# Contiguous operands for TensorE, v turned on the chip, and a new instruction order in a fused attention and gated-MLP kernel

## The chip, the cores and the metric

One core of a Trainium2 chip; the runs were made on four chips, so kernels are compared by their ratio to the kernel before in the same rounds. The metric is the device time of one execution, in microseconds (us), median of several runs. The kernel before takes 230.99 us (229.94 to 232.09, 3 runs).

## The reference, cut to what matters

```python
# q, k, v: (8 batches, 8 heads, 576, 64), fp32
scores = scale * q @ k^T                     # heads 0-3: band of 32; heads 4-7: band of 32 in steps of 4
attn   = softmax(where(mask, scores, -1e9))
x      = concat_heads(attn @ v)              # (8, 576, 512)
h      = gelu_tanh(x @ w_in)                 # 512 -> 1024
u, v_  = split(h)                            # 512 and 512
v_n    = (v_ - mean) / sqrt(var + 1e-6) * g_ln
v_s    = w_sg @ v_n + b_sg                   # "gating", over the 576 positions
out    = x + (u * v_s) @ w_out               # the residual is x itself
```

Of the kernel before, what the change touches and what calls it, by code (L numbers as in the profile page):

```python
# [11 lines left out]
FP32 = mybir.dt.float32  # L12
# [13 lines left out]
def _masks() -> np.ndarray:  # L26
    out = np.zeros((KB, 2, S), dtype=np.float16)
    p = np.arange(KB)[:, None]
    for a in range(NB):
        j = QB * a - HALO + p  # L30
        i = QB * a + np.arange(QB)[None, :]
        out[:, 0, QB * a:QB * a + QB] = (j >= 0) & (i >= j) & (i - j < 32)
    u = np.arange(128)[None, :]
    main = (u >= p) & (u - p < 32)
    i, j = 128 + np.arange(16)[None, :], 96 + p % 48
    tail = [(p // 48 == r) & (i >= j) & (i - j < 32) for r in range(2)]
    out[:, 1] = np.concatenate([x for r in range(2) for _ in range(2) for x in (main, tail[r])], axis=1)
    return out
# [3 lines left out]
ew iLQP:1 iLKP:1 iLQD:0 R:1:0:0 iLKD:0 R:1:0:1 w:27@2 S:1:0:1@0,1 iLQP:0 iLKP:0 iMSK iLVP:0 iLVH:0 iLVD:0  # L42
iLVT:0:1 iLVT:0:0 iLWV S:1:0:0@2,3 iLQD:1 iLWSG R:0:1:0 R:0:1:1 R:0:0:0 E:1:0:1:1 E:1:0:0:0 E:1:0:1:0
R:0:0:1 iLKD:1 S:0:1:1@1,2 E:1:0:0:1 S:0:1:0@0,3 E:0:1:0:1 E:0:1:1:1 M:0:3 E:0:1:1:0 E:0:1:0:0 iID iLWU
M:1:0 M:1:1 M:0:2 S:0:0:1@3,2 S:0:0:0@1,0 E:0:0:0:1 E:0:0:1:0 iBG AS:1:0@0 E:0:0:1:1 M:0:1 LN:1:0 iLKD:2
E:0:0:0:0 VC:0 AS:0:1@3 M:0:0 w:5@2 AS:0:0@2 w:3@1 AV:0:0:1@0 LN:0:0 LN:0:1 EX:0:0 EX:0:1 gw AV:0:0:0@1
NX:0:0:0 NX:0:0:1 w:4@2 AV:0:1:1@2 iLQD:2 AV:0:1:0@3 NX:0:1:0 NX:0:1:1 zv:0:4@1 R:1:1:0 Gz:0:2 st:0:4
zv:0:2@0 zv:0:3 Gz:0:1 zv:0:0@3 iLQP:2 sc:0 sa:0 rs:0:2 st:0:2 st:0:3 zv:0:1 Gz:0:0 ew st:0:1 st:0:0 R:1:1:1
WP:0:0 WP:0:1 w:13@1 W:0:2@2 S:1:1:1@1,0 E:1:1:1:1 rs:0:0 E:1:1:1:0 rs:0:1 vn:0:4 W:0:4@3 WC:0:2 iLKP:2
S:1:1:0@2,0 WC:0:4 E:1:1:0:0 vn:0:1 E:1:1:0:1 gw vn:0:0 W:0:0@3 zu:0:0@1 W:0:1@2 WC:0:0 M:1:3 WC:0:1 W:0:3@0  # L50
zu:0:2@3 Gu:0:2 M:1:2 vn:0:3 vn:0:2 WC:0:3 BG R:2:1:0 Gu:0:0 zu:0:1@2 Gu:0:1 zu:0:3@3 R:2:1:1 Gu:0:3 ew
AS:1:1@1 LN:1:1 sgr:0:1@2,0 sgu:0:1 EX:1:0 EX:1:1 VS:0:1 sgu:0:3 VS:0:3 sgr:0:0@3,1 sgu:0:2 VS:0:2 R:2:0:1
GA:0:2 w:2@2 S:2:1:1@2,0 E:2:1:1:1 sgu:0:0 E:2:1:1:0 GA:0:1 S:2:1:0@1,0 E:2:1:0:1 E:2:1:0:0 R:2:0:0 w:6@2
S:2:0:0@2,0 iLVH:1 iLVP:1 GA:0:3 VC:1 VS:0:0 GA:0:0 AV:1:0:1@1 E:2:0:0:0 E:2:0:0:1 NX:1:0:1 iLWO M:2:2 M:2:3
iLVT:1:0 AV:1:0:0@3 S:2:0:1@2,0 E:2:0:1:0 M:2:0 E:2:0:1:1 out:0:0@1 out:0:1 iLVT:1:1 O:0:0 out:0:4@2 O:0:2
M:2:1 NX:1:0:0 AS:2:0@0 LN:2:0 iLVD:1 AV:1:1:0@3 AS:2:1@1 LN:2:1 AV:1:1:1@2 EX:2:1 out:0:2@0 NX:1:1:0
NX:1:1:1 zv:1:0@3 iLVT:2:1 zv:1:1 EX:2:0 gw Gz:1:0 zv:1:2@1 zv:1:3 Gz:1:1 iLKP:3 out:0:3 R:3:0:1 iLVT:2:0
iLVD:2 st:1:1 O:0:1 st:1:0 zu:1:2@2 iLVP:2 iLVH:2 Gu:1:2 zv:1:4@3 iLQP:4 iLKD:4 st:1:2 Gz:1:2 iLKP:4 rs:1:0
st:1:3 vn:1:1 st:1:4 AV:2:1:1@1 NX:2:1:1 VC:2 vn:1:0 AV:2:1:0@0 zu:1:3@2 iLQD:3 zu:1:0@3 sc:1 sa:1 iLQP:3
AV:2:0:0@1 NX:2:1:0 rs:1:1 iLKD:3 NX:2:0:0 Gu:1:3 rs:1:2 iLVT:3:0 AV:2:0:1@0 zu:1:1@2 Gu:1:1 NX:2:0:1  # L60
zv:2:4@1 iLVH:3 vn:1:3 R:4:1:1 vn:1:2 R:4:0:1 R:4:0:0 zv:2:2@0 Gz:2:2 zv:2:3 Gu:1:0 iLVP:3 Gz:2:1 st:2:2
zu:2:1@2 zv:2:0@1 zv:2:1 Gz:2:0 vn:1:4 st:2:3 zu:2:0@3 Gu:2:0 zu:2:3@0 Gu:2:3 R:3:0:0 Gu:2:1 R:3:1:1
zu:2:2@1 sgr:1:0@3,0 Gu:2:2 ew sgu:1:0 st:2:4 R:3:1:0 S:4:0:1@2,1 E:4:0:1:0 VS:1:0 st:2:0 sgu:1:2 VS:1:2
E:4:0:1:1 iD:0:2 GA:1:0 sgr:1:1@3,2 sgu:1:3 iD:0:1 VS:1:3 GA:1:2 S:3:1:0@1,0 sgu:1:1 rs:2:1 GA:1:3 VC:3
E:3:1:0:1 E:3:1:0:0 iLVT:4:1 sc:2 iLVD:3 VS:1:1 iLVT:3:1 sa:2 GA:1:1 S:4:0:0@2,0 E:4:0:0:1 E:4:0:0:0 iLQD:4
st:2:1 S:3:1:1@1,3 E:3:1:1:1 E:3:1:1:0 out:1:2@0 S:3:0:1@2,3 M:4:1 iD:0:0 rs:2:0 M:3:3 vn:2:1 vn:2:0 iLVH:4
iLQD:5 M:3:2 out:1:3 rs:2:2 vn:2:2 iLVP:4 vn:2:4 vn:2:3 iLQP:5 iLKD:5 E:3:0:1:1 S:3:0:0@1,3 E:3:0:1:0
E:3:0:0:1 E:3:0:0:0 M:3:1 out:1:0@2 M:3:0 out:1:1 M:4:0 O:1:1 AS:3:1@3 R:4:1:0 O:1:0 sgr:2:0@1,0 LN:3:1
iLKP:5 EX:3:1 sgu:2:0 AS:3:0@2 VS:2:0 AV:3:1:1@3 LN:3:0 sgu:2:2 NX:3:1:1 VS:2:2 EX:3:0 AV:3:0:0@2 AS:4:0@1
LN:4:0 out:1:4@3 NX:3:0:0 O:1:2 AV:3:1:0@0 NX:3:1:0 AV:3:0:1@1 NX:3:0:1 VC:4 GA:2:2 sgr:2:1@3,2 sgu:2:1  # L70
S:4:1:0@0,1 VS:2:1 EX:4:0 E:4:1:0:1 E:4:1:0:0 R:5:0:0 GA:2:1 sgu:2:3 GA:2:0 S:4:1:1@3,1 E:4:1:1:1 VS:2:3
E:4:1:1:0 gw zv:3:2@0 R:5:0:1 GA:2:3 M:4:2 zv:3:3 Gz:3:1 zv:3:0@1 zv:3:1 Gz:3:0 iD:1:2 iD:1:0 zv:3:4@3
iD:1:1 M:4:3 AV:4:0:0@2 Gz:3:2 ew NX:4:0:0 iLVH:5 AV:4:0:1@0 iLVD:4 NX:4:0:1 AS:4:1@1 LN:4:1 out:2:2@3
R:5:1:0 R:5:1:1 st:3:4 st:3:3 S:5:0:1@2,0 out:2:3 iLVT:4:0 E:5:0:1:1 iLVT:5:1 iLVD:5 out:2:0@1 iLQD:6
E:5:0:1:0 EX:4:1 O:2:1 sc:3 S:5:1:0@0,2 st:3:1 E:5:1:0:0 iD:2:1 iLQP:7 st:3:0 E:5:1:0:1 out:2:1 AV:4:1:1@3
O:2:0 NX:4:1:1 sa:3 rs:3:2 out:2:4@0 AV:4:1:0@2 O:2:2 iLKD:7 NX:4:1:0 rs:3:0 S:5:0:0@1,3 iD:2:2 E:5:0:0:1
E:5:0:0:0 st:3:2 rs:3:1 iLVP:5 iLVT:5:0 zu:3:0@0 S:5:1:1@2,3 zv:4:2@1 iLKD:6 E:5:1:1:1 M:5:1 M:5:0 zv:4:0@3
vn:3:0 iD:2:0 vn:3:4 vn:3:2 vn:3:1 R:7:0:0 E:5:1:1:0 gw zv:4:3 M:5:2 M:5:3 vn:3:3 Gu:3:0 Gz:4:1 zu:4:0@2
Gu:4:0 zv:4:1 Gz:4:0 zu:3:3@0 Gu:3:3 zv:4:4@1 Gz:4:2 ew st:4:3 st:4:0 st:4:4 iLQP:6 iLKP:6 sgr:3:0@2,3 sc:4
st:4:1 iLVD:6 AS:5:1@0 AS:5:0@1 LN:5:0 LN:5:1 EX:5:1 EX:5:0 gw iLQD:7 rs:4:0 sgu:3:0 VS:3:0 sgu:3:2 sa:4  # L80
st:4:2 VS:3:2 rs:4:2 zu:3:2@1 GA:3:0 Gu:3:2 VC:5 sgr:3:1@0,2 sgu:3:1 VS:3:1 sgu:3:3 VS:3:3 zu:3:1@3 Gu:3:1
GA:3:2 AV:5:1:1@1 AV:5:1:0@0 iLVT:6:1 AV:5:0:1@2 NX:5:1:1 iLVD:7 NX:5:1:0 vn:4:4 AV:5:0:0@3 NX:5:0:1
zu:4:3@1 zu:4:2@0 Gu:4:3 iLVT:7:0 zu:4:1@2 NX:5:0:0 Gu:4:1 Gu:4:2 GA:3:1 zv:5:2@1 zv:5:3 zv:5:0@3 zv:5:1
rs:4:1 Gz:5:0 iLKP:7 vn:4:1 vn:4:3 R:6:0:1 GA:3:3 out:3:2@2 vn:4:0 R:6:1:1 Gz:5:1 out:3:3 O:3:1 R:6:1:0
zu:5:1@0 zv:5:4@3 Gu:5:1 out:3:4@1 iLVT:7:1 vn:4:2 R:6:0:0 st:5:0 Gz:5:2 ew R:7:1:0 st:5:2 st:5:4 sc:5
S:6:0:0@2,0 E:6:0:0:0 E:6:0:0:1 O:3:2 st:5:3 out:3:0@3 out:3:1 O:3:0 st:5:1 R:7:1:1 rs:5:0 sa:5 sgr:4:1@2,0
sgu:4:3 VS:4:3 sgu:4:1 VS:4:1 S:6:1:1@1,3 E:6:1:1:0 E:6:1:1:1 gw zu:5:3@0 zu:5:0@2 iLVT:6:0 rs:5:2 Gu:5:0
GA:4:1 rs:5:1 vn:5:4 GA:4:3 vn:5:1 vn:5:3 sgr:4:0@1,3 sgu:4:2 VS:4:2 vn:5:2 vn:5:0 GA:4:2 sgu:4:0 VS:4:0
zu:5:2@2 Gu:5:3 sgr:5:1@0,3 sgu:5:1 Gu:5:2 ew S:6:0:1@2,1 E:6:0:1:1 GA:4:0 VS:5:1 sgu:5:3 E:6:0:1:0 R:7:0:1
M:6:1 out:4:2@0 VS:5:3 iLVP:6 S:6:1:0@1,2 iD:3:2 iLVH:6 out:4:3 M:6:0 GA:5:1 E:6:1:0:0 out:4:0@3 E:6:1:0:1  # L90
VC:6 out:4:1 iD:3:1 iD:3:0 M:6:3 GA:5:3 O:4:1 O:4:0 sgr:5:0@1,2 M:6:2 AS:6:1@0 LN:6:1 sgu:5:0 S:7:0:1@3,0
VS:5:0 sgu:5:2 EX:6:1 GA:5:0 E:7:0:1:0 S:7:1:1@1,3 E:7:0:1:1 E:7:1:1:1 VS:5:2 out:4:4@0 O:4:2 E:7:1:1:0
AS:6:0@2 LN:6:0 iLVH:7 iLVP:7 AV:6:1:0@3 GA:5:2 EX:6:0 iD:4:0 out:5:0@0 S:7:1:0@1,2 E:7:1:0:1 iD:4:2 iD:4:1
NX:6:1:0 AV:6:0:0@3 NX:6:0:0 out:5:1 E:7:1:0:0 S:7:0:0@2,3 VC:7 M:7:3 M:7:2 E:7:0:0:1 M:7:1 E:7:0:0:0 O:5:0
M:7:0 out:5:2@1 out:5:3 AV:6:1:1@3 O:5:1 NX:6:1:1 AV:6:0:1@2 NX:6:0:1 out:5:4@0 O:5:2 AS:7:0@3 AV:7:0:1@1
AV:7:0:0@0 AS:7:1@2 LN:7:0 EX:7:0 LN:7:1 EX:7:1 gw zv:6:0@3 zv:6:1 Gz:6:0 NX:7:0:1 NX:7:0:0 AV:7:1:0@2
AV:7:1:1@1 NX:7:1:0 NX:7:1:1 zv:6:2@0 st:6:0 st:6:1 rs:6:0 zv:6:3 zv:7:2@2 Gz:6:1 st:6:2 st:6:3 vn:6:1
zv:6:4@1 Gz:6:2 vn:6:0 zv:7:4@3 zv:7:3 rs:6:1 vn:6:2 st:6:4 vn:6:3 Gz:7:1 Gz:7:2 st:7:3 st:7:4 sc:7 zu:7:3@0
zv:7:0@1 zv:7:1 Gz:7:0 st:7:1 sa:7 st:7:0 zu:7:2@2 Gu:7:2 rs:7:0 zu:7:0@3 zu:6:3@1 Gu:7:3 zu:6:1@2 Gu:6:3
Gu:6:1 zu:6:0@0 zu:6:2@1 Gu:6:0 st:7:2 Gu:7:0 sc:6 sa:6 rs:6:2 vn:6:4 zu:7:1@2 rs:7:1 rs:7:2 sgr:6:1@0,3  # L100
vn:7:0 vn:7:2 Gu:7:1 vn:7:1 sgu:6:1 VS:6:1 Gu:6:2 vn:7:3 sgr:6:0@2,1 vn:7:4 sgu:6:3 VS:6:3 GA:6:1 sgu:6:0
# [8 lines left out]
def kernel(  # L110
# [110 lines left out]
    def ld_mask():  # L221
        nc.sync.dma_start(masks, MSK.ap())
# [335 lines left out]
```

## The kernel before: the parts that the change and the argument touch

Positions are kept in residue order (position modulo 4 first), since the dilated heads need it. The order of all instructions is one long list of short names (the plan), played from left to right; each engine is given its own instructions in that order. `E` is an exp, `M` a mask product, `AV` attention times v, `S` the scores, `vn` a norm, `sgr`/`sgu` the gating, `w:n` are n filler matmuls of zeros, `@2,3` names the PSUM slots.

```python
def E(b, g, hf, x):                      # g = 0: band heads, g = 1: dilated heads
    nc.scalar.activation(PTb[...][:, :, HS*hf:HS*hf+HS], live["pss", b, g, hf][x][:, :, 0:HS], AF.Exp, scale=0.125)

def AV(b, g, x):                         # band heads: PT is read in steps of four
    ...
        nc.tensor.matmul(o[:, :, 24*(s%3):24*(s%3)+24], v_, PT[:, QB*s:QB*s+QB].rearrange("p (m u) -> p u m", u=4), ...)

def out_(b, ti):                         # the residual: a matmul onto the identity, every second column of PSUM
    ...
        nc.tensor.matmul(po[:, ti % 2, 256*(g4//2):256*(g4//2)+256].rearrange("p (w x) -> p x w", x=2)[:, g4 % 2, :],
                         xT[:, g4, ts], ident16, start=False, stop=(g4 == 3))

def vn(b, ti):                           # norm, on VectorE
    nc.vector.tensor_scalar(dst, vv, mean, rstd, AO.subtract, AO.mult)

def ld_vp(b):                            # v in rows of 64 elements, one queue (SyncE)
    nc.sync.dma_start(vst[HALO:KB], v[b][0:4].rearrange("h (a p) d -> p (h a) d", p=QB))
```

The softmax here doesn't subtract the row's maximum and nothing guards it: scores larger than these inputs give would overflow.

## Time and profile before

| | before |
|---|---|
| time | 230.99 us |
| span of the profiled run | 229.2 us |
| TensorE / VectorE / ScalarE busy | 209.8 / 171.2 / 147.3 us |
| fillers among TensorE's work | 60 matmuls, 16.8 us |
| first large projection, first gating matmul | 29.0 us, 46.1 us |

The first fence is the table of stretches of the kernel before (length, then busy time of PE, PEld, DVE, ACT and POOL, clock, DMA share, GB/s); the second is ScalarE's largest group up to the first gating matmul at 46.08 us.

```profile
40.00:60.00 20.00, 19.07 (x289) 12.87 (x288) 18.29 (x30) 13.79 (x21) 5.28 (x9) 0.93 0.90 140
60.00:80.00 20.00, 20.00 (x277) 12.44 (x274) 15.72 (x30) 13.49 (x19) 5.44 (x12) 1.00 0.77 126
80.00:100.00 20.00, 19.30 (x312) 12.38 (x311) 18.42 (x35) 16.84 (x25) 10.90 (x18) 1.00 0.98 180
```

```profile
L292 ACT ACTIVATE PT<-pss 128x576 f16<-128x576 f32 x16 | 9.4, 654 | 13.4 <-PE pss L288 13.3
```

Sixteen exps, those of two batches, are done before the first gating, and ScalarE still stood 13.4 us for scores. They had room there.

### The profile page before, as it was taken

How to read it: one execution, taken by the hardware profiler on the slowest of the kernel's cores; microseconds unless marked ns; L12 is line 12 of the kernel's file. 1: busy time of each engine (PE TensorE's matmuls, PEld its weight loads, DVE VectorE, ACT ScalarE, POOL GpSimd, SP SyncE). 2: the span in 40 equal slices, each digit the busy share in tenths (PEclk: the TensorE clock that was granted, in tenths of full speed). 3: DMA queues.
4: the chain of work that ended last, by engine and by line, in shares of the span. 5: the costliest groups of instructions: out<-in, count | busy, mean ns of one | idle time of the engine just before them, and what ended most of it. 6: DMA issues, size and time to landing. Idle time of an engine off the chain costs nothing.

```text
span 229.2 us, 6969 instructions
## 1 busy us (share of the span) xinstructions
PE 209.8 (92%) x3020; PEld 131.5 (57%) x3020; DVE 171.2 (75%) x314; ACT 147.3 (64%) x201; POOL 67.8 (30%) x131
## 2 busy tenths in 40 slices
PE   7627896998999999999999999999999999999990
PEld 2223444765657566565565676666656655766650
DVE  2487478898768999899879989988955668686400
ACT  2068658678685598778979973756788785721231
POOL 8244057602017061922029364050000003420000
PEclk9955999799999999999999999999999999999998
DMA  8999997993917979998849999026076430000354
GB/s 157 205 216 212 208 205 136 171 158 57 219 22 102 209 220 171 142 190 124 246 69 223 215 216 195 8 44 212 3 125 159 159 114 3 0 1 3 114 169 128
DMA packets 45326, 31.68 MB, mean 138 GB/s; under 512 B 30048, under 2 KB 36704, under 8 KB 45296
## 3 DMA queue, kind: packets, MB, share of 16 engines
q0 software_dynamic: 13984, 14.95, 41.6%
q1 hardware_dynamic: 31312, 16.29, 29.4%
q8 instruction: 23, 0.38, 0.7%
q14 instruction: 7, 0.06, 0.1%
HBM read 36.75 MB, written 9.44 MB: 202 GB/s over the span
## 4 chain that ended last, share of the span: by engine, by line
PE 71%; DMA 9%; DVE 9%; ACT 4%; POOL 2%; issue 2%; ACTq 1%; DVEq 0%; POOLq 0%
PE po L465 13%; PE pg L443 11%; PE pz L367 11%; PE pu L421 10%; PE po L468 6%; DMA qkp<-in_k_dram 5%; PE pss L288 4%; DMA qkd<-in_k_dram 4%; PE pav L310 4%; PE psu L338 3%; DVE vs L449 2%; PE po L475 2%; PE pg L436 2%; PE pav L321 2%; PE pb L507 2%
## 5 line engine op out<-in xcount | busy, mean ns | idle before, releaser
L292 ACT ACTIVATE PT<-pss 128x576 f16<-128x576 f32 x64 | 38.0, 651 | 24.7 <-PE pss L288 24.6
L421 PE MATMUL pu<-xT,w_in 128*128 128x288 f16 x256 | 35.4, 292 | 0.0
L443 PE MATMUL pg<-wsgT,vn 128*128 128x288 f16 x256 | 35.4, 287 | 0.0
L465 PE MATMUL po<-w_out,gat 128*128 128x512 f16 x128 | 33.5, 384 | 0.0
L449 DVE SCALAR_TENSOR_TENSOR vs<-pg,g_col,b_bc 128x576 f16<-128x576 f32 x32 | 25.5, 804 | 9.3 <-PE pg L443 9.2
L367 PE MATMUL pz<-w_in,xT 128*128 128x512 f16 x128 | 29.7, 380 | 0.0
L421 PEld LDWEIGHTS <-w_in 128*128 128x128 f16 x256 | 25.0, 100 | 7.9 <-issue 0.3
L487 ACT COPY osb<-po 128x1024 f32<-128x1024 f32 x16 | 16.2, 1016 | 19.9 <-PE po L468 18.7
L443 PEld LDWEIGHTS <-vn 128*128 128x128 f16 x256 | 23.2, 98 | 9.6 <-issue 3.8
L426 ACT ACTIVATE u<-pu 128x576 f16<-128x576 f32 x32 | 19.9, 650 | 12.7 <-PE pu L421 12.5
L406 POOL TENSOR_SCALAR rs<-mv 128x2 f32<-128x2 f32 (+1 forms) x24 | 7.0, 292 | 67.2 <-DVE mv L393 62.4
L297 DVE TENSOR_TENSOR PT<-PT,masks 128x1152 f16<-128x1152 f16 x32 | 22.8, 748 | 1.4 <-ACT PT L292 1.3
L388 DVE BATCH_NORM_STATS2 st<-vv 128x6 f32<-128x512 f32 x32 | 21.5, 671 | 3.2 <-ACT vv L378 3.1
L378 ACT ACTIVATE vv<-pz 128x1024 f32<-128x1024 f32 x16 | 16.3, 1025 | 9.3 <-PE pz L367 7.2
L412 DVE TENSOR_SCALAR vn<-vv,mv,rs 128x512 f16<-128x512 f32 (+1 forms) x40 | 19.2, 507 | 3.2 <-POOL rs L407 3.2
L367 PEld LDWEIGHTS <-xT 128*128 128x128 f16 x128 | 12.0, 99 | 13.3 <-issue 0.6
L468 PE MATMUL po<-ident,xT 128*128 128x128 f16 x128 | 19.2, 304 | 0.0
L352 DVE TENSOR_TENSOR xT<-pav,rsum 128x576 f16<-128x576 f32 x16 | 11.6, 752 | 8.6 <-PE pav L310 5.0
L407 POOL TENSOR_TENSOR rs<-rs,mhalf 128x2 f32<-128x2 f32 (+1 forms) x24 | 17.4, 723 | 2.0
L507 PE MATMUL pb<-zeros 128*128 128x512 f16 x60 | 16.8, 433 | 1.2 <-DVE zeros L170 1.2
L465 PEld LDWEIGHTS <-gat 128*128 128x128 f16 x128 | 12.3, 107 | 9.2 <-issue 0.4
L468 PEld LDWEIGHTS <-xT 128*128 128x128 f16 x128 | 13.2, 118 | 7.6
(68 smaller groups left out, 311.5 us busy)
## 6 DMA issues: line engine op xcount, KB each, us to landing
vst<-in_v_dram SPq DMA_DIRECT2D x8, 576.0 KB, 9.0
qkp<-in_q_dram POOLq DMA_DIRECT2D x8, 288.0 KB, 5.9
qkp<-in_k_dram POOLq DMA_DIRECT2D x8, 288.0 KB, 8.0
qkd<-in_q_dram POOLq DMA_DIRECT2D x8, 288.0 KB, 6.3
qkd<-in_k_dram POOLq DMA_DIRECT2D x8, 288.0 KB, 7.5
vm<-in_v_dram POOLq DMA_DIRECT2D x8, 256.0 KB, 6.7
out_dram<-osb SPq DMA_DIRECT2D x8, 256.0 KB, 3.5
out_dram<-osb SPq DMA_DIRECT2D x8, 224.0 KB
```

Of the source, the lines that this page charges most:

```text
L292: nc.scalar.activation(PTb[4 * (b % 2) + 2 * g + x][:, :, HS * hf:HS * hf + HS], live["pss", b, g, hf][x][:, :, 0:HS], AF.Exp, scale=0.125)
L297: nc.vector.tensor_tensor(PT, PT, masks[:, p // 2, :].unsqueeze(1).broadcast_to([KB, 2, S]), AO.mult)
L367: nc.tensor.matmul(pz[:, ti % 2, :], xT[:, g4, 128 * ti:128 * ti + 128], w_in16[:, g4, DH:DFF], start=(g4 == 0), stop=(g4 == 3))
L388: nc.vector.bn_stats(s, vvs[(3 * b + i) % 4][:, c, :])
L412: nc.vector.tensor_scalar(vns[b % 2][:, ti, 0:n], vvs[(3 * b + i) % 4][:, c, 0:n], live["mv", b, i][:, c, 0:1], live["rs", b, i][:, c, :], ...
L421: nc.tensor.matmul(pu[:, j, 0:HS], w_in16[:, g4, 128 * ph:128 * ph + 128], xT[:, g4, HS * j:HS * j + HS], start=(g4 == 0), stop=(g4 == 3))
L426: nc.scalar.activation(us[b % 2][:, ph, :].rearrange("p (j w) -> p j w", j=2), live.pop(("pu", b, ph))[:, :, 0:HS], AF.Gelu_apprx_tanh)
L443: nc.tensor.matmul(pv[:, j, 0:HS], vns[b % 2][:, kp, 128 * ph:128 * ph + 128], wsgT16[:, kp, HS * j:HS * j + HS], start=False, stop=(kp == 3))
L449: nc.vector.scalar_tensor_tensor(vs.rearrange("p (j w) -> p j w", j=2), live.pop(("pg", b, ph))[:, :, 0:HS], g_col[:, ph:ph + 1], b_bc.rea ...
L465: nc.tensor.matmul(po[:, ti % 2, :], gat[:, ph, ts], w_out16[:, ph, :], start=(ph == 0), stop=False)
L468: nc.tensor.matmul(po[:, ti % 2, 256 * (g4 // 2):256 * (g4 // 2) + 256].rearrange("p (w x) -> p x w", x=2)[:, g4 % 2, :], xT[:, g4, ts], i ...
L507: nc.tensor.matmul(pb[:, 0, :], zeros[:, 0:128], zeros, start=True, stop=True)
```

## The change

Its intent: make every operand of TensorE contiguous (the residual's output, the band heads' PT), load v of the first two batches in whole rows instead of short pieces and turn it on the chip, make the first loads smaller, share the norms between VectorE and ScalarE, and play all of it in a new order. The diff, cut to its core:

```diff
 def E(b, g, hf, x):
+    if g == 0:                                        # exp writes residue order
+        dst = dst.rearrange("p h (u m) -> p h u m", u=4)
+        src = src.rearrange("p h (m u) -> p h u m", u=4)
 def AV(b, g, x):
-                        PT[:, QB * s:QB * s + QB].rearrange("p (m u) -> p u m", u=4),
+                        PT[:, HS * (s // 3):HS * (s // 3) + HS].rearrange("p (u m) -> p u m", u=4)[
+                            :, :, 24 * (s % 3):24 * (s % 3) + 24],
 def out_(b, ti):
-                nc.tensor.matmul(po[:, ti % 2, 256 * (g4 // 2):256 * (g4 // 2) + 256].rearrange(
-                        "p (w x) -> p x w", x=2)[:, g4 % 2, :], xT[:, g4, ts], ident16, ...)
+                nc.tensor.matmul(po[:, ti % 2, 128 * g4:128 * g4 + 128], xT[:, g4, ts], ident16, ...)
+def WO():                                             # w_out's columns permuted once, on GpSimd
+def O(copy):                                          # the eviction undoes the order; on ScalarE or VectorE
+def ld_v(b, g):                                       # whole rows, two batches only
+    dma(vraw(b, g), v[b][4 * g:4 * g + 4].rearrange("h (p w) d -> (h p) (w d)", p=32))
+def RV(b, g): turn(...)                               # 32 x 32 transposes on VectorE
+def VT(b, g): ... 224 small matmuls in all            # and on TensorE
+def VK(copy): ...                                     # their evictions
+def nm(b, i): ... ; vnA: nc.scalar.activation(dst, src, AF.Identity, bias=-mean*rstd, scale=rstd)   # 17 of 40 norms
-    out = np.zeros((KB, 2, S), ...)                   # masks: 1152 columns
+    return np.concatenate([band, band & (p >= HALO), main] + tail, axis=1)   # 352, spread by 5 copies
-    nc.sync.dma_start(b_row, moe_b_sg.unsqueeze(0).to_broadcast([128, S]))
+    nc.sync.dma_start(b_row, moe_b_sg.unsqueeze(0))   # one row, spread by two fp32 matmuls
-PLAN = """ew iLQP:1 iLKP:1 iLQD:0 R:1:0:0 ... w:27@2 S:1:0:1@0,1 ...      # two batches' scores first; 60 fillers
+PLAN = """ew iLQD:0 iLKD:0 iLKP:0 iLQP:0 iMSK MX ... w:12@1 PB@0 ...      # batch 0 alone first; 16 fillers
```

## The prediction

> **What bounds the kernel now.** I read the page first, then the table of stretches, then the chain of work that ended last, then TensorE's timeline in the steady part.
>
> From the page, parts 1, 2 and 5:
>
> ```profile
> PE 209.8 (92%) x3020; PEld 131.5 (57%) x3020; DVE 171.2 (75%) x314; ACT 147.3 (64%) x201; POOL 67.8 (30%) x131
> ...
> PE   7627896998999999999999999999999999999990
> ...
> DVE  2487478898768999899879989988955668686400
> ...
> DMA  8999997993917979998849999026076430000354
> ...
> L507 PE MATMUL pb<-zeros 128*128 128x512 f16 x60 | 16.8, 433 | 1.2 <-DVE zeros L170 1.2
> ```
>
> TensorE is busy 92% of the span, and its row holds nines from the eleventh slice on. The pb row is no work at all: 60 matmuls of zeros, 16.8 us[...]. So real TensorE work is about 193 us of 229.2. DVE is the second engine, in the nines in many slices. DMA is close to full in the first ten.
>
> From the table of busy time by stretch:
>
> ```profile
> 0.00:10.00 10.00, 7.93 (x27) 3.07 (x27) 2.87 (x13) 1.28 (x1) 5.57 (x13) 1.00 0.94 178
> 10.00:20.00 10.00, 3.65 (x168) 2.92 (x168) 8.88 (x11) 5.69 (x11) 3.61 (x6) 0.60 1.22 213
> ...
> 100.00:140.00 40.00, 40.00 (x701) 25.92 (x700) 36.43 (x68) 32.46 (x44) 16.29 (x32) 1.00 0.97 185
> 140.00:180.00 40.00, 40.00 (x543) 25.40 (x542) 31.52 (x56) 29.20 (x41) 3.90 (x10) 1.00 0.47 102
> ```
>
> The columns are the length, then busy time of PE, PEld, DVE, ACT and POOL, the granted clock, the DMA share and GB/s. There are two kernels in one. Up to about 46 us it waits for loads: 0 to 10 us is filling only, and 10 to 20 us has 3.65 us of TensorE work at a clock of 0.60. After that TensorE has no idle time (40.00 of 40.00, twice), with DVE at 91% and 79% beside it.
>
> The chain of waits agrees: its longest piece is one load, later pieces are nearly all TensorE.
>
> ```profile
> 4.11 12.11 DMA qkp<-in_k_dram
> ...
> 209.96 0.86 PE po L465 x4
> 210.82 0.44 PE po L468 x4
> ```
>
> Four matmuls of 512 columns take 0.86 us, 215 ns each; four of 128 columns onto the identity (L468, the residual) take 0.44, 110 ns each. A quarter of the columns costs half the time. TensorE's timeline shows the same of the band heads:
>
> ```profile
> 173.10 0.69 PE L338 MATMUL psu<-PT,ones 128*32 128x288 f16 x8
> 173.60 0.31 PE L321 MATMUL pav<-PT,vm 128*32 128x128 f16 x8
> 173.73 0.19 PE L325 MATMUL pav<-PT,vt 128*32 128x32 f16 x4
> 173.75 0.29 PE L321 MATMUL pav<-PT,vm 128*32 128x128 f16 x8
> 173.87 0.19 PE L325 MATMUL pav<-PT,vt 128*32 128x32 f16 x4
> 173.99 1.04 PE L465 MATMUL po<-w_out,gat 128*128 128x512 f16 x4
> ...
> 175.82 0.71 PE L310 MATMUL pav<-PT,vp 128*32 128x96 f16 x24
> 176.47 1.04 PE L465 MATMUL po<-w_out,gat 128*128 128x512 f16 x4
> ```
>
> I take the distance from one group's start to the next, since the ends are modelled. Attention times v for the dilated heads (L321 and L325, 24 matmuls, contiguous PT) goes from 173.60 to 173.99, 0.39 us. The band heads' (L310, also 24, same number of columns, PT read in steps of four) goes from 175.82 to 176.47, 0.65 us. The sums psu: 0.50 us for the band (173.10 to 173.60); the same timeline has 0.36 for the dilated (168.99 to 169.35).
>
> [...] the L468 matmuls, which write every second fp32, run at half rate. [...] No row here has contiguous 128-column writes with fresh full weights; the pw matmuls, 72 columns with a fresh weight load each, start 55 ns apart[...]. [...]
>
> **The change part by part.**
>
> TensorE. The residual matmuls now write contiguous columns; w_out's columns are permuted once to match, and the eviction undoes the order. 32 groups of four go from 0.44 to about 0.24 us (four times 60): -6.4 us. The small last tile (8 groups, 0.31 us each from start to start) goes to about half: -1.2. Exp now writes PT in residue order, so L310 reads contiguous runs: 16 x (0.65 - 0.39) = -4.2 us. psu of the band: 8 x (0.50 - 0.36) = -1.1. Sum -12.9 us. Batch 0's eighth of that (1.6 us) falls into the front, which is counted below, so -11.3 on the steady path.
>
> Added on TensorE: turning v takes 48 or 64 small matmuls four times, 224 in all. Score matmuls with 128-column weights start about 13 ns apart (32 in 0.42 us, 171.90 to 172.32), so 224 x 13 = 2.9 us; three of the four fall before TensorE is saturated, the fourth (48) puts +0.7 on the path. The bias broadcast by two fp32 matmuls is in the front. Fillers go from 60 to 16; they filled waits, so alone this gains nothing.
>
> VectorE. Gone: 16 norms of 535 ns and one of 394 (-9.0 us), 4 evictions of wsg at 756 (-3.0). New: 3 copies of v of 1536 elements (about 1.0 each at the norm's slope of 0.55 ns an element: +3.0), 5 output evictions (2 large at 1.2, 3 small at 0.4: +3.6), 4 transposes of v (+5.3), 2 evictions of turned v (+2.2), masks and memsets (+1.6). Net about +3.7, to 175 us. But 9.1 of the new time is in the front or just after it; from batch 2 on, 13 moved norms (-7.0) balance the +6.6. So DVE keeps its steady load, in a shorter stretch.
>
> ScalarE. New: 17 norms[...]: +13; evictions of wsg +2.6 and of turned v +5.2; two table loads of 1283 ns: +2.6. Gone: 5 v copies of 1477 (-7.4), 5 output evictions (-3.2). Net +13, to 160 us. The strided PSUM read of exp and the evictions I cost at nothing[...]. No row shows it; if wrong, 32 exps double their streaming part (0.48 us each), +15 us.
>
> The front. Before, first loads share the DMA engines with 288 KB of masks, 760 KB of v in short pieces and the 288 KB broadcast bias, and two batches' band heads come first. In the new order the four q and k tiles of batch 0 come first, masks shrink to 352/1152, the bias to one row, and v comes as two 288 KB loads of whole rows. The software queue moved 14.95 MB in 41.6% of the span, 157 GB/s, so a 288 KB tile alone takes about 1.9 us: [...]landings near 5, 7, 9 and 11 us against 8 to 16 before. First scores come near 9 us instead of 11.1. Exps, masks, turning v, attention and normalisation follow; I put the first large projection at 25 us, where it began at 29.0. It then has wsg and both halves of w_in arrive earlier, so I expect the gating matmuls (46.4 us before) about 4.5 us sooner.
>
> The end. The last instruction is a small eviction instead of a 1.02 us one: -0.7.
>
> Sum: 231.0 - 11.3 + 0.7 - 4.5 - 0.7 = 215.2. TensorE will not stay without a gap when 7% of its work goes and DVE and ACT keep theirs, so I add 1.5 us of new waits: 216.7.
>
> **The rivals.**
>
> A: DVE becomes the bound. For it: 36.43 of 40 us at 100 to 140, and its steady work does not fall. Against: 128 us over 60 to 223, so 85% now and about 92% in a stretch shorter by 12. It would keep half of the steady gain away: 221 to 223.
>
> B: ScalarE becomes it, through strided exps. For it: +13 us anyway and two-way traffic between Gelu and exp tables. Against: 160 of 215 is 74%. With the +15 it would be near 81% and delay every mask: 220 to 224.
>
> C: the front is bound by something other than loads, such as ScalarE (8 exps, 3 v evictions, logs, a table load and a 2.25 us wsg copy before the first projection). Then its 4.5 us vanish: 221. Or the reverse: removing 16.8 us of fillers shows that most waits can be packed, the front gains 9 us: 212.
>
> [...]
>
> **Range and chances.** The main term is read off like-for-like pairs in the trace and is nearly certain to appear as TensorE busy time; what is unsure is how much of it the other engines give back and the size of the front. I predict 216.7 us, 8 in 10 within 210.5 and 223.5. Faster by 2% means below 226.4, for which nearly all terms would have to fail: 0.95. Within 2%: 0.04. Slower: 0.01.
>
> **What would show it right or wrong.** Right: L468 groups at 0.22 to 0.26 us in the chain, L310 start-to-start near 0.39, psu of the band near 0.36; TensorE busy near 187 us including some 4 us of fillers; the exp row of the band still near 651 ns; gating of batch 0 from about 42 us. Wrong: exps of the band near 1.1 us (B); TensorE idle of several us between 60 and 210 with VectorE as releaser (A); first large projection still at 28 us or later (C)[...]. If TensorE's busy time falls as summed and the span does not, my error is in the waits, not in the costs.

## The result, and the profile after

The changed kernel takes 223.68 us (223.65 to 224.7, 3 runs) against 230.99. The ratio is 0.9697 (95% interval 0.9614 to 0.978). Ratios are the mean time of one kernel's fast runs over that of the kernel before's fast runs of the same rounds, so they are not quite the ratio of the medians. Below I turn ratios into us by 231, and compare experiments by them; the changed kernel then stands at 224.0. Its own interval is about 2 us each way, so differences under 2 us are weak.

It is faster, as predicted, but I had put 216.7 with a range of 210.5 to 223.5. I expected 14.3 us and got 7.0 to 7.3.

The page after, parts 1, 4 and 5:

```profile
PE 197.4 (89%) x3204; PEld 124.9 (56%) x3204; DVE 175.2 (79%) x320; ACT 156.8 (70%) x222; POOL 77.5 (35%) x154
...
PE 56%; ACT 28%; issue 4%; DVE 4%; DMA 3%; POOL 1%; SPq 0%; ACTq 0%; DVEq 0%
...
L368 ACT ACTIVATE PT<-pss 128x576 f16<-128x576 f32 x64 | 37.7, 652 | 15.9 <-PE pss L360 15.6
```

The same row of the chain's shares, and the same exps, in the page of before:

```profile
PE 71%; DMA 9%; DVE 9%; ACT 4%; POOL 2%; issue 2%; ACTq 1%; DVEq 0%; POOLq 0%
...
L292 ACT ACTIVATE PT<-pss 128x576 f16<-128x576 f32 x64 | 38.0, 651 | 24.7 <-PE pss L288 24.6
```

And, of the changed kernel, the table of stretches where the one of before was shown:

```profile
40.00:60.00 20.00, 17.31 (x445) 10.93 (x445) 18.01 (x25) 17.35 (x27) 5.71 (x10) 0.91 0.56 85
60.00:80.00 20.00, 18.43 (x303) 11.29 (x301) 19.69 (x35) 16.99 (x25) 9.81 (x16) 1.00 1.08 180
80.00:100.00 20.00, 19.71 (x309) 12.38 (x308) 19.03 (x35) 18.51 (x26) 11.79 (x22) 1.00 0.99 176
```

From the chain of work that ended last, the pair that the prediction showed of before (0.86 and 0.44 us):

```profile
213.41 0.97 PE po L552 x4
214.38 0.22 PE po L555 x4
```

The costs of single operations came as predicted. The residual's four matmuls take 0.22 us instead of 0.44; exp is unmoved at 652 ns (651 before), although half of them now read PSUM in steps of four (what they write stays in one run). But from 40 to 80 us TensorE is now busy 35.74 of 40 us where it was 39.07 (2.06 of these were fillers; now there are none), and ScalarE holds 28% of the chain where it held 4%. TensorE got cheaper work and new gaps.

One more number prepares the experiments. I added up the TensorE work done by a given moment, each matmul at its typical distance in the changed kernel to the next of its kind, leaving out fillers, the turning of v and the bias broadcast, so that all kernels count the same 175.9 us of useful work:

```
useful TensorE work done by (us)       40     50     60    100    150    last matmul starts
before                                11.3   20.0   26.1   62.3  108.6   222.7
before, contiguous (first of two)     11.2   18.9   25.6   63.2  112.1   214.4
before, contiguous (second)           12.6   21.7   29.0   65.7  114.7   211.8
changed (first of two)                14.1   19.6   26.7   63.2  110.2   216.1
changed (second)                      14.5   20.9   28.9   64.9  111.6   214.7
```

(The second run of each pair has another issue of the last output transfers and is otherwise the same.) Against the contiguous kernel of the old order, the changed order leads by 2 to 3 us at 40 us, has no lead at 50, is 0 to 0.8 us behind at 100 and 2 to 3 us at 150.

### The profile page after: what moved, and what is told of

It is laid out like the page before. It is cut to its first block, busy times and chain, and to the rows that moved or that the text cites.

```text
span 222.9 us, 7406 instructions
## 1 busy us (share of the span) xinstructions
PE 197.4 (89%) x3204; PEld 124.9 (56%) x3204; DVE 175.2 (79%) x320; ACT 156.8 (70%) x222; POOL 77.5 (35%) x154
## 4 chain that ended last, share of the span: by engine, by line
PE 56%; ACT 28%; issue 4%; DVE 4%; DMA 3%; POOL 1%; SPq 0%; ACTq 0%; DVEq 0%
PE pg L530 12%; PE pu L508 10%; PE pz L443 10%; PE po L552 9%; ACT PT L368 8%; ACT u L513 3%; PE pss L360 3%; ACT L601 3%; DMA g_row<-in_moe_g_ln_dram 3%; ACT vv L454 2%; ACT vn L498 2%; PE po L555 2%; ACT L598 2%; PE pg L523 2%; PE psu L414 2%
## 5 line engine op out<-in xcount | busy, mean ns | idle before, releaser
L530 PE MATMUL pg<-wsgT,vn 128*128 128x288 f16 x256 | 36.8, 294 | 0.1
L508 PE MATMUL pu<-xT,w_in 128*128 128x288 f16 x256 | 34.4, 286 | 0.1
L552 PE MATMUL po<-w_out,gat 128*128 128x512 f16 x128 | 32.9, 379 | 0.5 <-POOL w_out L231 0.3
L443 PE MATMUL pz<-w_in,xT 128*128 128x512 f16 x128 | 31.0, 387 | 1.3 <-ACT osb L575 1.2
L530 PEld LDWEIGHTS <-vn 128*128 128x128 f16 x256 | 23.7, 100 | 10.6 <-issue 4.0
L508 PEld LDWEIGHTS <-w_in 128*128 128x128 f16 x256 | 24.5, 98 | 7.8
L572 ACT COPY osb<-po 128x1024 f32<-128x1024 f32 x14 | 14.0, 1008 | 15.0 <-PE po L555 15.0
L443 PEld LDWEIGHTS <-xT 128*128 128x128 f16 x128 | 12.2, 99 | 14.3 <-issue 2.2
L454 ACT ACTIVATE vv<-pz 128x1024 f32<-128x1024 f32 x16 | 16.2, 1024 | 4.8 <-PE pz L443 4.7
L474 POOL COPY st<-st 64x6 f32<-64x6 f32 x16 | 5.2, 326 | 40.3 <-DVE st L467 39.9
L552 PEld LDWEIGHTS <-gat 128*128 128x128 f16 x128 | 11.3, 97 | 9.3 <-issue 0.6
L541 DVE TENSOR_TENSOR gat<-u,vs 128x576 f16<-128x576 f16 x32 | 14.6, 477 | 0.3
L555 PEld LDWEIGHTS <-xT 128*128 128x128 f16 x128 | 9.8, 98 | 7.6
L417 ACT ACTIVATE rsum<-psu 128x576 f32<-128x576 f32 x16 | 10.2, 659 | 5.4 <-PE psu L414 5.3
## 6 DMA issues: line engine op xcount, KB each, us to landing
out_dram<-osb SPq DMA_DIRECT2D x8, 224.0 KB, 2.7
```

Source lines behind the costliest of these rows:

```text
L443: nc.tensor.matmul(pz[:, ti % 2, :], xT[:, g4, 128 * ti:128 * ti + 128], w_in16[:, g4, DH:DFF], start=(g4 == 0), stop=(g4 == 3))
L454: nc.scalar.activation(vv, pz, AF.Gelu_apprx_tanh)
L508: nc.tensor.matmul(pu[:, j, 0:HS], w_in16[:, g4, 128 * ph:128 * ph + 128], xT[:, g4, HS * j:HS * j + HS], start=(g4 == 0), stop=(g4 == 3))
L530: nc.tensor.matmul(pv[:, j, 0:HS], vns[b % 2][:, kp, 128 * ph:128 * ph + 128], wsgT16[:, kp, HS * j:HS * j + HS], start=False, stop=(kp == 3))
L541: nc.vector.tensor_tensor(gats[b % 2][:, ph, :], us[b % 2][:, ph, :], live.pop(("vs", b, ph)), AO.mult)
L552: nc.tensor.matmul(po[:, ti % 2, :], gat[:, ph, ts], w_out16[:, ph, :], start=(ph == 0), stop=False)
```

## The experiments

### Does the instruction supply stop TensorE?

The trace after shows TensorE standing in the middle of a run of matmuls, with no releaser that the trace shows:

```profile
21.98 0.40 PE L397 MATMUL pav<-PT,vm 128*32 128x128 f16 x6
25.95 0.29 PE L397 MATMUL pav<-PT,vm 128*32 128x128 f16 x2 [3.57 <-issue]
```

This is after 350 matmuls or 700 instruction rows, a multiple of 256 if some 63 to 68 rows come before the first matmul (a fitted number), and instruction packets of 16 KB (25 in the whole trace, for 6408 matmuls and weight loads) come about 6.5 us apart there (at 16.7, 23.4, 29.6 and 36.5 us), while the loads fill the DMA engines (a share of 1.16 from 20 to 30 us). To tell it from a hidden wait, I shifted the rows by 124:

```diff
-w:12@1
+t:64@1 w:10@1          # 64 matmuls of 32 columns ahead of ten fillers
```

> The changed kernel with 64 tiny matmuls (32x32 on zeros, two instruction rows each) put ahead of the fillers and 2 large fillers fewer, in TensorE's idle time before the first scores: 124 rows more ahead of all real work, nothing else. Theory I (instruction supply): in the changed kernel TensorE stands still for 3.6 us at 22.4 us in the middle of one tile's matmuls, with no releaser, about 700 rows into its stream, and the 25 packets of the instruction queue have 16 KB, so 256 rows each; the waits are for the next 256 rows. Then the 3.6 us hole at that instruction goes (or moves by 124 rows and shrinks below 1.5 us), the first large projection starts near 25 us instead of 28.7, and the time falls from 223.7 to about 220.5 (219.5 to 222). Theory II (the hole is a hidden wait for a load or for memory traffic): it stays at the same matmul, between the 46th and 47th of the dilated heads' second attention product, 3 to 4 us long, and the time stays within 1 us of 223.7.

Measured 227.64 us (ratio 0.9857, 0.9815 to 0.9898). The stop left its matmul and appeared at two new ones, again 256 rows apart: after 350 matmuls, as in the changed kernel, and 128 matmuls later.

```profile
21.03 0.59 PE L383 MATMUL pav<-PT,vp 128*32 128x96 f16 x20 [1.71 <-issue]
...
27.32 0.25 PE L330 MATMUL pvt<-ident,vn 32*48 32x32 f16 x4 [2.62 <-issue]
```

So the stop goes with the 256 rows and not with that matmul; that it waits there for instructions is my reading. But shifting it cures nothing: the two stops here end 6.3 us apart, and the time rose by 3.7 us.

### The contiguous operands alone

The kernel before, its order kept, with only exp in residue order, contiguous residual and permuted w_out:

```diff
+        if g == 0: dst, src = (residue order)          # E, AV, AS and masks as in the change
-                nc.tensor.matmul(po[...every second column...], xT[:, g4, ts], ident16, ...)
+                nc.tensor.matmul(po[:, ti % 2, 128 * g4:128 * g4 + 128], xT[:, g4, ts], ident16, ...)
-out:0:0@1
+WO out:0:0@1
```

> The kernel before, in its own order, with the contiguous accesses alone: exp writes residue order, the residual matmuls write contiguous columns, w_out permuted once. Theory P (my prediction's main term): TensorE's work falls by about 11 us as in the changed kernel and, since TensorE is without idle time from 60 to 223 us, most of it shows: 220 to 222 us, as fast as the changed kernel or faster, TensorE idle in the middle still small. Theory S (the other engines pace as soon as TensorE is shorter): ScalarE and VectorE keep their work, TensorE gains idle time of 5 us or more in the middle, and the time is 225 to 228.

Measured 222.32 us (ratio 0.9613, 0.9564 to 0.9663): -8.9 us. From its page:

```profile
PE 199.8 (91%) x3020; PEld 124.0 (56%) x3020; DVE 170.8 (77%) x314; ACT 146.3 (66%) x201; POOL 70.9 (32%) x133
```

TensorE is busy 10.0 us less than before. One part of the change carries at least the whole gain. All the rest together nets about +2 us here, which is within the noise of the changed kernel's own ratio; a pair measured further below gives 3.1. The counterpart, the changed kernel with the strided residual put back:

```diff
-                nc.tensor.matmul(po[:, ti % 2, 128 * g4:128 * g4 + 128], xT[:, g4, ts], ident16, ...)
+                nc.tensor.matmul(po[...every second column...], xT[:, g4, ts], ident16, ...)
```

> The changed kernel with the residual matmuls writing every second fp32 again and plain output evictions; TensorE's work rises by the 6.9 us that it fell by (68 to 115 ns for 128 of them, 45 to 73 for 32). Theory P (TensorE's work sets the time): 229 to 231 us. Theory S (ScalarE paces the middle, TensorE has slack there): only the part after about 150 us, where TensorE has no idle time, shows, about 40% of it: 226 to 227.

Measured 227.44 us (ratio 0.9869, 0.9836 to 0.9902), +4.0 us for about 6.9 us of TensorE work: that part shows by more than half in the changed order, too, though by less than in the old one (8.9 of 10.0). The result lies between the two that the expectation named.

### v in short pieces in the new order

```diff
-iLV:0:0 ... RV:0:0 VT:0:0 VK:0:0:0 ...     # whole rows, turned
+iLVP:0 iLVH:0 ... VC:0 ...                 # v of batches 0 and 1 as in the kernel before
```

> The changed kernel with v of the two first batches loaded as for all others (short pieces from HBM, one ScalarE cast for the band heads) and not turned on chip: 224 matmuls or 448 instruction rows fewer, 4 transposes and 8 evictions fewer, some 2 MB of short pieces more in the front. Theory I (instruction supply in the front): the hole of 3.6 us goes, ScalarE and VectorE have less to do, and what is left is later loads; 219 to 223. Theory L (loads bound the front, as the change assumes): the late v and weights cost more than the turning did; first large projection after 30 us and 225 to 229.

Measured 235.45 us (ratio 1.0133; its profile fell in the slow state, so only the direction counts). Attention waits 13.5 us for v. So the new front needs v in whole rows. That the old front did not is explained by the last experiment below.

### Which engine's load paces the changed kernel?

Useless work of known size was put in at eight places between about 50 and 100 us, on one engine at a time, and at twelve places between about 100 and 195 us:

```diff
+dA     # ScalarE: copy of 576 fp32, 0.65 us  |  VectorE: product of 576 fp32, 0.75 us
+w:3@n  # TensorE: three fillers, 0.65 us
```

> The changed kernel with 8 useless ScalarE copies of 576 fp32 (about 0.65 us each, 5.2 us) spread between about 50 and 100 us. If ScalarE paces that stretch, nearly all of the 5.2 us shows in the time (+4 to +5); if it does not, below +1.5. To be read beside the two runs that add as much to VectorE and to TensorE at the same places.

> The same 8 places, with useless VectorE products of 576 fp32 (about 0.75 us each, 6 us). If VectorE paces the stretch, +4 to +6; if ScalarE or TensorE does, below +2.

> The same 8 places, with three filler matmuls of 512 columns each (about 0.65 us, 5.2 us together). If TensorE still paces the stretch, +4 to +5; if it waits for ScalarE or VectorE there, its waits hide most of it: below +2.

> The changed kernel with 12 useless VectorE products (0.75 us each, 9 us) spread over 100 to 195 us. There TensorE is busy 97% and VectorE falls off after 180 us. If TensorE paces this part: below +3 us. If VectorE does: +6 to +9.

> The same 12 places with three filler matmuls each (7.8 us together). If TensorE paces this part: +6.5 to +8. If its waits for others can hide them: below +4.

| added | where | work added | median us | ratio (95%) | against 224.0 |
|---|---|---|---|---|---|
| ScalarE | 50-100 | 5.2 us | 224.25 | 0.9725 (0.9647-0.9802) | +0.6 |
| VectorE | 50-100 | 6.0 us | 227.51 | 0.9865 (0.979-0.9941) | +3.9 |
| TensorE | 50-100 | 5.2 us | 228.17 | 0.99 (0.983-0.9971) | +4.7 |
| VectorE | 100-195 | 9.0 us | 226.15 | 0.9718 (0.9649-0.9787) | +0.5 (2 fast runs of 4; medians: +2.5) |
| TensorE | 100-195 | 7.8 us | 233.22 | 1.0096 (1.0039-1.0152) | +9.2 |

TensorE's load sets the time in both stretches. ScalarE's load does not between 50 and 100 us, although ScalarE holds 28% of the chain over the whole span: a large share of the chain does not make an engine the one that sets the pace. Of VectorE's load 3.9 of 6.0 us showed in the early stretch, so I formed the theory that VectorE paces it.

### Moving norms between the two engines

First all 17 norms back to VectorE, then six more norms and a copy of v to ScalarE, then the same 17 norms to ScalarE in the contiguous kernel of the old order:

```diff
-vnA:0:4 nm:0:2 ...                   +vn:0:4 ...                      # norms back on VectorE
-vn:0:3 vn:1:0 ... vn:1:4 VCD:3       +vnA:0:3 vnA:1:0 ... VC:3        # more on ScalarE
-vn:0:4 vn:0:1 ...  (old order)       +vnA:0:4 nm:0:2 ...              # the change's split, old order
```

> The changed kernel with all 17 norms back on VectorE as single instructions of 0.54 us (ScalarE about 13.7 us less, VectorE about 9 us more, the small preparing instructions dropped), in the changed kernel's order. If ScalarE is what paces the stretch from 40 to 110 us (most of TensorE's waits there end on it), the time falls by 2 to 4 us, to about 220. If VectorE paces, it rises by 3 to 6 us, to 227 to 230. If TensorE alone sets the pace, it stays within 1 us of 223.7.

> The changed kernel with six more norms (one of batch 0, all five of batch 1) and one copy of v moved from VectorE to ScalarE, all between about 45 and 85 us: VectorE 4.2 us less, ScalarE about 6 us more. VectorE paces the stretch from about 28 to 110 us (my theory now): the time falls by 2 to 4 us, to about 220. ScalarE paces (the wait attribution): it rises by 3 or more. TensorE alone: within 1 us of 223.7.

> The kernel before with contiguous accesses (222.3 us) and the change's 17 norms on ScalarE, in the old order, without the new front, the turning of v and the new evictions: VectorE about 9 us less than there. If VectorE paces after the contiguous accesses as much as in the changed kernel, where 17 norms were worth 9.9 us, the time falls to 214 to 217. If the old order leaves VectorE free, within 2 us of 222. If ScalarE's queue is what delays, above 224.

| | median us | ratio (95%) | difference |
|---|---|---|---|
| norms back on VectorE | 233.54 | 1.0098 (1.0001-1.0194) | +9.3 |
| more norms on ScalarE | 233.06 | 1.0084 (1.004-1.0128) | +8.9 |
| old order, 17 norms on ScalarE | 234.16 | 1.0134 (1.0067-1.0201) | +12.0 against contiguous alone |

The first run alone would have looked like a proof that VectorE paces (9 us of work, 9.3 us of time). The second refutes that reading: taking work off VectorE costs as much, and my expectation had the sign wrong. The traces show why. I laid the starts of the same matmuls of two kernels side by side. With the norms back on VectorE the two differ by less than 2 us, and by -0.4 just before 100 us; then the delay jumps by 4.5 at 102 us and by 3.4 up to 126 us. Part of such a jump is clock: with the norms back, TensorE's granted clock was 0.50 from 102.4 to 105.8 and from 129.7 to 133.1 us, right behind the waits, and I can't part the two. At the first jump, TensorE waits for norms, and between the norms VectorE plays a transpose of 1.44 us:

```profile
99.54 0.30 PE L527 MATMUL pg<-wsgT,vn 128*128 128x288 f16 x1 [1.52 <-DVE vn L497]
101.20 2.68 PE L527 MATMUL pg<-wsgT,vn 128*128 128x288 f16 x15 [1.37 <-DVE vn L497]
```

```profile
98.57 0.91 DVE L497 TENSOR_SCALAR vn<-vv,mv,rs 128x512 f16<-128x512 f32 x2
99.39 1.44 DVE L294 STREAM_TRANSPOSE kTd<-qkd 128x320 uint32<-128x320 uint32 x2
100.68 0.47 DVE L497 TENSOR_SCALAR vn<-vv,mv,rs 128x512 f16<-128x512 f32 x1
```

With more norms on ScalarE there is a jump at 38 us (a second one of about 4 us comes at 74 to 80 us, where TensorE waits 2.67 us for a normalised tile from ScalarE). Here, too, the clock was 0.50 from 37.8 to 44.6 us and from 78.7 to 85.5. A norm stands 3.16 us for its statistics, and behind it in the queue stands the eviction of w_sg that TensorE waits for:

```profile
37.70 0.81 ACT L496 ACTIVATE vn<-vv,nm,rs 128x512 f16<-128x512 f32 x1 [3.16 <-POOL nm L487]
38.42 1.16 ACT L283 CAST wsgT<-pw 128x576 f16<-128x576 f32 x2
```

```profile
39.09 0.45 PE L278 MATMUL pw<-ident,gat 72*64 72x72 f16 x8 [3.61 <-ACT wsgT L283]
```

So, as I read these traces, what such a move costs is the place in the queue (and the stretch at a clock of 0.50 that came right behind these waits), and not the engine's load. Eight useless copies that nobody waits for cost ScalarE 0.6 us in all; at a jump a move costs some 4 us. No run kept the engine and changed the place alone, so this is read and not shown, and the +12.0 us in the old order were not traced to their places.

### Taking VectorE work away without moving it

The mask products of batches 1 to 3 were left out (12 of 0.745 us), in both orders. The output is wrong (relative error 0.55).

```diff
-M:1:0 M:1:1 ... M:3:3
```

> The changed kernel without the 12 mask products of batches 1 to 3 (0.745 us each, 8.9 us of VectorE between about 45 and 100 us; the output is wrong on purpose). If VectorE paces that stretch, the time falls by 5 to 7 us, as 3.8 of 6 us showed when work was added. If it is the order of the queues and not VectorE's load, by less than 2.5.

> The same 12 products left out of the kernel before with contiguous accesses (222.3 us; output wrong on purpose), where VectorE has 7 us less to do in the first 100 us. If VectorE's load is what takes the changed kernel's lead, this run gains clearly less than the one in the changed order: 0 to 3 us. If both gain alike, VectorE's load paces both orders and does not explain the loss of the lead.

Measured: in the changed order 221.89 us (ratio 0.9592, 0.9538 to 0.9646), -2.4 us; in the old order, contiguous, 220.94 us (ratio 0.9488, 0.9429 to 0.9546), -2.9 us against contiguous alone. Both gain about a third of the 8.9 us, and alike. These gains are small against the noise: against the two kernels with a divided end (next but one section), they are 1.3 and 0.5 us, and the second has 2 fast runs of 4. VectorE's load matters little in either order and does not explain why the new one lost its lead. The theory fell.

### Is it the turning of v?

The changed kernel without the turning: no transposes of v, no 224 matmuls, no evictions; GpSimd fills the tiles with ones, and the loads stay. Its output is wrong, which doesn't matter for the time.

```diff
-RV:0:0 VT:0:0@0,2 VK:0:0:0 VK:0:0:1 ...
+vz:0:0 ...                             # memset of the tiles on GpSimd
```

> The changed kernel with the turning of v of batches 0 and 1 taken out: no transposes, no 224 small matmuls and no evictions of them; GpSimd fills the three tiles with ones in their places (the loads stay; the output is wrong on purpose). On record I put +0.7 us on the turning, so by that theory the time falls by 1 us or less, to about 223. If the turning (4.4 us of TensorE, 5.2 of VectorE and 5.2 of ScalarE work and 448 instruction rows in the first 55 us) is what eats the front's lead, it falls by 4 to 6 us, to about 218 to 219, and the stall of 3.5 us at an instruction block's end shrinks or goes.

Measured 222.73 us (ratio 0.9658, 0.9613 to 0.9704): -0.9 us. That is within the noise; it agrees with my +0.7 for the turning, and the 4 to 6 us of the rival in the expectation were not seen. (This run has a stop of its own, 2.45 us for no visible reason at 55.1 us, and a clock of 0.50 from 42.1 to 48.9 us, which may hide a part.) The 3.57 us stop is gone, and its time with it only in part: now TensorE waits for ScalarE's 2.27 us rearrangement of w_sg, which the stop had covered. The first fence is TensorE's timeline, the second the chain of work.

```profile
18.38 0.20 PE L398 MATMUL pav<-PT,vt 128*32 128x32 f16 x4
21.89 0.42 PE L277 MATMUL pw<-ident,gat 72*128 72x72 f16 x4 [3.31 <-ACT gat L267]
```

```profile
18.27 1.28 ACT L602
...
19.57 2.27 ACT gat L267
```

This run also had an earlier front and lost it. Its useful work is 17.4 us at 40 us, 3 more than the changed kernel's; at 60 it is 27.6, no more than theirs.

### Where the lead goes

Compare what had been done before the first gating matmul: the scores of before up to 46.08 us, then those of the changed kernel up to 39.07 us.

```profile
L288 PE MATMUL pss<-qTd,kTd x128: 164/212/304, 14.5 to 39.3; 32*128 32x128 f16 x64, 32*128 32x16 f16 x64
L288 PE MATMUL pss<-qTp,kTp x96: 198/225/273, 11.1 to 18.6; 32*128 32x96 f16 x96
```

```profile
L360 PE MATMUL pss<-qTd,kTd x64: 164/192/228, 8.7 to 10.5; 32*128 32x128 f16 x32, 32*128 32x16 f16 x32
L360 PE MATMUL pss<-qTp,kTp x48: 231/273/274, 12.4 to 13.5; 32*128 32x96 f16 x48
```

Twice 112 matmuls before, 112 after. Gating comes 7 us earlier because the second batch's scores, exps and masks were put behind it. ScalarE's row says the same (sixteen exps before, eight after):

```profile
L368 ACT ACTIVATE PT<-pss 128x576 f16<-128x576 f32 x8 | 4.6, 656 | 8.9 <-PE pss L360 8.8
```

The other eight then stand in the busy stretch. From the chain of the changed kernel, and TensorE's timeline beside it:

```profile
41.69 1.28 ACT L601
...
42.98 4.55 ACT PT L368 x8
```

```profile
43.68 0.44 PE L360 MATMUL pss<-qTp,kTp 32*128 32x96 f16 x22 [0.29 <-ACT PT L368]
...
45.40 0.49 PE L360 MATMUL pss<-qTd,kTd 32*128 32x128 f16 x30 [0.31 <-ACT PT L368]
...
47.58 0.40 PE L523 MATMUL pg<-wsgT,vn 64*128 64x288 f16 x3 [0.27 <-ACT PT L368]
```

A table load of 1.28 us and eight exps, one after the other, with TensorE waiting for them in small pieces. Not all of the lost 2 to 3 us are these waits: 48 small matmuls of the turning (0.73 us, not counted as useful) stand there, too. Without the turning the eight exps come 4.5 us earlier (38.51 to 43.06 us) and the lead goes again, but in that run the clock was 0.50 just then (42.1 to 48.9 us). All this is read from traces; no run moved these eight exps back alone, so it is a reading and not shown by an experiment. The useless ScalarE work began after this place, so it does not speak against it.

There is a rival that I had left out: TensorE's granted clock in the front. The stretch of 20 to 30 us and the first large projection, first before, then changed:

```profile
20.00:30.00 10.00, 8.91 (x141) 4.02 (x138) 5.72 (x10) 7.05 (x11) 2.65 (x5) 0.89 1.13 208
28.97 3.63 PE L367 MATMUL pz<-w_in,xT 128*128 128x512 f16 x16
```

```profile
20.00:30.00 10.00, 5.63 (x164) 3.99 (x156) 5.64 (x9) 4.23 (x6) 3.52 (x6) 0.55 1.16 209
28.69 1.86 PE L443 MATMUL pz<-w_in,xT 128*128 128x512 f16 x4
```

The projections start 216 ns apart before, and 427 in the changed kernel, whose clock stood at 0.50 from 21.1 to 31.3 us. In all fast profiles of the changed order the full clock is back only at 28 to 34 us; in five of six of the old order it is by 22 to 25. Useful matmuls at half clock fill 11.6 us of TensorE's time in the changed kernel and 7.2 in the kernel before, and 10.6 and 3.7 in the second runs of the two orders in the table; if all of it ran at half rate, half of the difference, 2 to 3.5 us, is lost (an estimate). Less filler work was left (16 matmuls for 60, the last at 15.8 us); whether the clock stayed low for that is open, since no run put them back. The clock does not explain the loss between 40 and 50 us, though: in these second runs both are at full clock from 32 us on, and the lead still goes.

One more piece can be placed: at 109.4 us TensorE stands 1.15 us for a small output eviction that waits on ScalarE behind a table load (1.16 in two other runs of the changed order, not in the old one). No run isolated it, either.

### The end, and the two orders side by side

The last batch's output transfers issued from two queues:

```diff
+            q = nc.scalar if b == 7 and c else nc.sync
-                    nc.sync.dma_start(d, ...)
+                    q.dma_start(d, ...)
```

> The changed kernel with the last batch's output transfers issued from two queues (SyncE and ScalarE) instead of one. In its chain the last nine issues take 4.5 us one after the other. If their serial issue is what made the end no shorter, -1.5 to -2.5 us; if the transfers themselves or their completion set it, within 0.5 us.

> The kernel before with contiguous accesses and the last transfers from two queues. Against the run of the changed order with the same tail on the same chip: if the rest of the change (first loads in whole rows, turned v, norms on ScalarE, new order) is worth nothing, the two are within 1.5 us; if it was a gain hidden by chance, the changed order is 3 us or more faster; if a loss, this one is 1 to 2 us faster. The tail alone should take 1 us off 222.3.

Measured, 6 runs each: the changed order 222.96 us (ratio 0.9647, 0.9596 to 0.9698), the old order with contiguous operands 220.28 us (ratio 0.9511, 0.9462 to 0.9561). The intervals do not touch: by the ratios of fast runs the old order is 3.1 us faster. (The medians of all six differ by 2.7 us, the means by 1.8; two runs of the old order and none of the changed one were set aside as slow.) This old order with contiguous operands is the fastest correct kernel. That the divided issue did it is not shown. From the start of the last matmul to the end of the span it is 6.8 us in the changed kernel with and without it, and 6.3 and 5.9 in the old order; the other gains of the second run lie in the front, where nearly equal programs differ by 1 to 3 us from run to run (table above), and so do their slow stretches of the clock (0.51 and 1.00 from 40 to 45 us in the two of the old order).

### Smaller first loads in the old order

The contiguous kernel with the divided end, with the change's small masks and one-row bias, and both loads moved to the head of the SyncE queue:

```diff
-ew iLQP:1 iLKP:1 ... w:27@2 ... iMSK iLVP:0 iLVH:0 ... BG
+ew iMSK iBG iLQP:1 iLKP:1 ... MX w:23@2 PB@3 BG ... iLVP:0 iLVH:0
```

> The kernel before with contiguous accesses and the divided tail (220.3 us), with the change's smaller masks and one-row bias: 0.5 MB less to load in the first 45 us, at some 200 GB/s about 2.5 us. If loads bind the old front, -1 to -2.5 us, to about 218.5; if not, or if the five mask copies and the broadcast cost as much, within 1 us of 220.3.

Measured 233.68 us (ratio 1.0136, 1.0104 to 1.0169): +14.4 us, a miss in size and sign. The first fence is SyncE's queue in the kernel before, the second here, the third a line of its chain:

```profile
0.73 0.35 SPq L222 DMA_DIRECT2D masks<-band_masks  x1
1.13 0.44 SPq L190 DMA_DIRECT2D vst<-in_v_dram  x1
1.61 2.29 SPq L194 DMA_DIRECT2D vst<-in_v_dram  x1
```

```profile
2.41 1.29 SPq L241 DMA_DIRECT2D g_row<-in_moe_g_ln_dram  x4
3.74 0.34 SPq L188 DMA_DIRECT2D vst<-in_v_dram  x1
4.13 10.31 SPq L192 DMA_DIRECT2D vst<-in_v_dram  x1
```

```profile
4.13 30.16 DMA vst<-in_v_dram
```

By moving the bias ahead I had put v's load 2.6 us later. Before, v's short pieces were issued at 1.13 us, before the large loads of the other queue began to move (their first packets ran between 4.5 and 4.6 us), and 2429 packets of SyncE's queue ran in the first 8 us. Here they came when the other queue was busy, and from then on both queues advanced packet for packet (8 to 24 us: 2256 packets of the one, 2243 of the other), a short one for each long one. v landed at 34 us. This run so tests a place in a queue, not the smaller masks; these stay untested. It also explains the run with v in short pieces, where v was issued at 3.90 us and its second part took 24.5 us to land.

## Why the prediction was wrong

By its own sum, -12.9 us came from contiguous operands and -1.4 from all else (-14.3 in all). The runs give -8.9 and +1.9, the second a weak number (+3.1 in the pair). Two steps failed: all else, first of it the front, gained nothing in the end, and of the contiguous operands two thirds showed.

**"Sum -12.9 us": mechanism right, size off.** Summed from start to start over the whole trace, residual matmuls went from 14.69 to 8.74 us (115 to 68 ns each; predicted -6.4, got -5.95), the band heads' attention from 9.36 to 6.05 (24.4 to 15.8 ns each; -4.2, got -3.3), psu from 7.37 to 5.71 (-1.1, got -1.7). The costs so came within 1 to 2 us of the sum; the term alone showed 10.0 us of busy time and 8.9 of time. Within a group of four the residual's matmuls start 56 ns apart; my 60 was an estimate. The pw row, which I named for it, gave no support: these matmuls, 55 ns apart, ran at a clock of 0.50 (39.3 to 42.7 us); at full clock they start 32 to 33 ns apart (37.3 us). That 60 came near was luck as far as it rested on them. Rival B's strided exp did not come: 652 ns. That it would cost nothing was an estimate, too; the 0.48 us of rival B are 576 elements at the 0.83 ns an element between ScalarE's 386 and 1025 ns for 256 and 1024 elements.

**"The front -4.5": this step failed.** I took the first gating matmul as the measure. It did come 7 us earlier, more than I said. But a milestone is not work: half the score matmuls and eight exps had been put behind it. Measured in useful work the front won 2 to 3 us, and it was gone by 50 us, where TensorE waits for the second batch's exps. Rival C named a part of it rightly: the first large projection stayed at 28.7 us (29.0 before). The loads were not what held it: the four tiles landed at 5.6, 7.2, 9.0 and 10.2 us, close to my estimate. ScalarE's exps, evictions and logs, the stop of 3.57 us and the clock of 0.50 from 21.1 to 31.3 us did, as I read the trace, and the last two I had not thought of.

**"Turning v +0.7": agrees within noise.** Taking it out gave 0.9 us.

**"They filled waits, so alone this gains nothing" (the fillers): too simple.** The sum has no term for the clock, and after the change TensorE ran at a clock of 0.50 for longer in the front (useful matmuls at half clock fill 11.6 us against 7.2). The prediction's own sign, TensorE busy near 187 us with some 4 us of fillers, came at 197.4: fillers are 5.6 us, turning v 4.6 where 2.9 was summed, the bias broadcast 1.2 where nothing was; some 6 us are left, and half of those 11.6 us at half clock would be 5.8 (an estimate). So, by its last sentence, not only the waits were wrong.

**"DVE keeps its steady load" and "ScalarE +13, to 160 us": sums right (175.2 and 156.8 us), use wrong.** The cost of the 17 norms on ScalarE was an estimate; they took 13.0 us (16 of 0.81 and one of 0.59). I judged these engines, as in rivals A and B, by busy share (and A's is summed wrongly: 128 of 163 us are 79%, not 85%). Rival A's number came nearest, but its reason is not what the runs show: 8.9 us less VectorE work gains 2.4 us in the new order and 2.9 in the old. Moving norms cost 9 to 12 us in either direction; by the traces, what counted was whom each instruction makes wait in its queue.

**"The end -0.7": failed, small.** From the start of the last matmul to the end it was 6.5 us before and is 6.8 after.

**"1.5 us of new waits": too small.** Behind by 2 to 3 us at 150 us, after a lead of 2 to 3, the new order paid about 5. Some 2 to 3 of them are placed at 40 to 50 us. Of the others most, about 2 us, fall between 100 and 150 us, 1.15 of these at one wait at 109 us; the rest stays open. VectorE's load and the turning of v explain little of it, and no run isolated these pieces.

## What to carry to other kernels

Apply the part of a change that lowers the busiest engine's work by itself first, in the old order; here it was worth at least as much as the whole. Judge a new order by the work done at a moment, not by how early a milestone comes, since work may only have been put behind it. Moving norms cost 9 to 12 us here whichever engine got them, and as I read the traces what stood before and behind them in the queue decided it; so a move needs its own place, and a run that only moves it can measure the place as much as the engine. Look at the granted clock of each stretch, too, before a gap in time is put down to waits or to order.
